# Four edits near the end of a fused forward-and-backward block: staging tiles, the order of three norms, filler matmuls, PSUM banks

## The chip, the cores and the metric

The kernel runs on one core of a Trainium2 chip. The metric is the time of one execution on the device in microseconds; of several runs the median counts. One run was also recorded by the hardware profiler; its page and its trace are what the readings below use. PE is TensorE, DVE is VectorE, ACT is ScalarE, POOL is GpSimd, SP is SyncE, which only issues DMAs here.

## The reference

The reference runs one block forward and then its gradient. The block has two halves, each with a layer norm that is scaled and shifted by vectors made from a condition `c`.

```python
mod = (silu(c) @ w_mod)            # sa, ca, ga, sb, cb, gb: six vectors of 576
h = layernorm(x) * (1 + ca) + sa
x = x + ga * irfft2(rfft2(h) * (w_r + 1j * w_i))          # half A, 2048 x 576
h = layernorm(x) * (1 + cb) + sb
x = x + gb * (((h @ w_gate) * (h @ w_up)) @ w_down)       # half B, 4608 hidden
# outputs: x, and the gradients of A_x, w_r, w_i, w_gate, w_up, w_down, c, w_mod
```

All inputs and outputs are bfloat16. The 2048 rows are 16 tiles of 128, the 4608 hidden columns 36 blocks of 128. The Fourier transforms are done as matmuls with tables of sines and cosines.

## The kernel before

The program has these parts, in the order of the trace. All engines work through their own queues in order; a planner at compile time orders each queue by priorities and estimated due times, except where the program ties instructions together (`in_order`, or `behind`, which puts what is issued inside it after a given instruction of the same engine).

1. **The head** (up to L581): the forward transform, filter and inverse of half A, and in its gaps the product of `grad_out` and `w_down`, stored as `ghhT_d`.
2. **The gated loop** (L759 to L787): for each of the 36 blocks the two forward products (`gup`), the sums for the input gradient (`u8p`, added in SBUF by DVE at L751), and three weight-gradient products of an earlier block (`u57p`, `product`). Each of these 108 products is 2 x 16 matmuls; ACT copies it into one of four slots of the staging tile `so4`, and from there it is stored, or transposed by a DMA on SP's queue (L655) and then stored.
3. **The last two blocks** (L788 to L804): their sums come tile by tile (L791), 8 matmuls for each of 16 tiles, and `summed[t]` is DVE's last addition for tile t. Their six products are `held`: 48 of the 192 matmuls go between the sums (`lead`), 144 are left over as fillers. The sixth product, of block 35, uses the fourth slot of `so4` and the fifth product the third; both are transposed into the tiles `wo_l`.
4. **Stage 1** (`t1_norm`, `t1_turn`, `t1_cols`, `t1_rows`, 19 steps): the gradient of the second norm and the forward transform of the gradient. `t1_norm(t)` works on DVE and ACT (`norm_back`) and makes `gxf`, which PE turns in `t1_turn(t)` one step later. The norms of tiles 0, 1 and 2 are put behind `summed[8]`, `summed[11]` and `summed[14]` on DVE. After each `gx` store POOL's queue may carry a load for the last product: five tiles `wd` of 7, 7, 7, 7 and 8 blocks of `w_down`, and four `hl` tiles of stored activations (L1090 to L1098). These tiles lie in memory that the gated loop's tiles had before; a load waits until all tiles under it are done with.
5. **Stage 2** (`t2_...`, 24 steps): filter and its gradient. **Stage 3**, the inverse (`t3_rows`, `t3_cols`, `t3_norm`, 18 steps): the inverse transform and the gradient of the first norm; `t3_norm` adds column sums into `csD` and `csE`.
6. **The output product** `u3p` (L1263 to L1303): for each of 16 row tiles and each half of 288 columns 36 matmuls into one PSUM bank; ACT copies it to `ob`, DVE makes the output tile, POOL stores it. The first ten tiles' 720 matmuls are fillers; the last six tiles' follow. Behind tiles 8 to 13 stand six *sections* (`section`): PE spreads a vector (`spp`), ACT copies it (`dmb`, two buffers) and scales it five times, SP loads a part of `w_mod` (`wmj`, two buffers), and DVE multiplies the two (`pr7`). When all six are done, DVE makes `gcd` and PE the last product `gcp`.

`deal` (L882) writes PE's order through stages 1 to 3: after the matmuls of each step it takes `q` fillers from a list that begins with the 144 held matmuls and goes on with `u3p`: 16 a step in stage 1, 12 in stage 2, 20 in step 0 of stage 3 and 14 in each of its other steps. When the list is empty no more are taken; fillers left over follow in the planner's order.

PSUM has eight banks. In the last three stages three are `ps_fp`, three are `ps_cs` (tags `csA`, `csB`, `csC`; `csD` takes the bank of `csA`, `csE` that of `csC`), and two are `ps_u3`, in turn for `u3p`.

Of the kernel before, what the change touches and what calls it, by code (L numbers as in the profile page):

```python
# [9 lines left out]
FP32 = mybir.dt.float32  # L10
BF = mybir.dt.bfloat16
# [10 lines left out]
D = 576  # L22
DP = 640
# [75 lines left out]
def build(ctx, tc, A_x, A_w_r, A_w_i, B_w_gate, B_w_up, B_w_down, c_in, w_mod, grad_out,  # L99
          out_0, out_1, out_2, out_3, out_4, out_5, out_6, out_7, out_8):  # L100
    nc = tc.nc
# [46 lines left out]
    def traced():  # L148
        return len(nc.cur_bb.bb.instructions)
# [6 lines left out]
    def followed(mm, act):  # L156
        then_act[mm.ins.name] = act.ins
# [102 lines left out]
    with ExitStack() as hs:  # L260
        def pool(name, bufs, side="left", space=None, stack=hs):
            kw = dict(name=name, bufs=bufs, reuse_waits="tile")
            if space is not None:
                kw["space"] = space
            else:
                kw["side"] = side
            return stack.enter_context(tc.tile_pool(**kw))
# [315 lines left out]
    with ExitStack() as ms:  # L583
# [14 lines left out]
        def ghb(t):  # L598
            return acc(t).bitcast(BF)[:, 0:D]

        with ExitStack() as bs:
            FBW = 2
            FBT = 4
            def bpool(name, bufs, space=None):
                kw = {} if space is None else dict(space=space)
                return bs.enter_context(tc.tile_pool(name=name, bufs=bufs, reuse_waits="tile", **kw))
# [7 lines left out]
            sop = bpool("sop", 1)  # L614
# [10 lines left out]
            nc.gpsimd.memset(dgb_l[:], 0.0)  # L625
            pend = []
            NSO = 4
            so4 = sop.tile([128, NSO, DP], BF, name="so4")
            nc.gpsimd.memset(so4[:, :, D:DP], 0.0)
            nso = [0]  # L630
            late_sp, unstored = [], []

            def u57_items(sf, rhs_n, done):
                so = so4[:, nso[0] % NSO, :]
                nso[0] += 1
                items = []
                for h in range(2):
                    pw = []

                    def item(h, t, pw=pw):  # L640
                        if t == 0:
                            pw.append(u57ps.tile([128, 512], FP32, name="u57p", tag="x"))
                        mm = nc.tensor.matmul(pw[0][:, 0:288], lhsT=sf[:, t, :], rhs=rhs_n(t, h * 288, 288), start=(t == 0), stop=(t == NT - 1))  # L643
                        if t == NT - 1:
                            followed(mm, nc.scalar.copy(so[:, h * 288:(h + 1) * 288], pw[0][:, 0:288]))  # L645
                            if h == 1:
                                done(so)
                    items += [lambda h=h, t=t, item=item: item(h, t) for t in range(NT)]
                return items
# [89 lines left out]
            summed = {}  # L739
# [70 lines left out]
    with ExitStack() as ts:  # L810
# [9 lines left out]
        ps_cs = pool("ps_cs", 1, space=PSUM)  # L820
        ps_u3 = pool("ps_u3", 2, space=PSUM)
# [37 lines left out]
        def behind(insts):  # L859
            es = ExitStack()  # L860
            for i_ in insts:
                es.enter_context(tc.issue_after(i_))
            return es
# [18 lines left out]
        def deal(held, proj):  # L882
            more, seq, acts = held + proj, list(lead), scaled["2"][0:3]
            for n, (stage, k, ins) in enumerate(staged):
                last_ = len(seq)
                seq += ins
                steps = sum(x[:2] == (stage, k) for x in staged)
                at = sum(x[:2] == (stage, k) for x in staged[:n + 1])
                q = 16 if stage == 1 else 12 if stage == 2 else 20 if k == 0 else 14
                q = q * at // steps - q * (at - 1) // steps  # L890
                seq, more = seq + more[:q], more[q:]
                if stage == 1:
                    acts += [then_act[i_.name] for i_ in seq[last_:] if i_.name in then_act]
                    acts += scaled["2"][k + 2:k + 3] * (at == steps and k > 0)
            in_order(seq)
            in_order(acts)
# [56 lines left out]
        with ExitStack() as r1:  # L953
# [14 lines left out]
            def t1_norm(t):  # L968
                if t == 0:
                    nc.sync.dma_start(ga_h[:], modb_d[:, MGA, :])  # L970
                for k, src, tt in [("n2c", n2_d, 0)] * (t == 0) + [("n2c", n2_d, t + 1)] * (t < NT - 1) + [("yc", y_d, t)]:
                    ld[k, tt] = c1.tile([128, D], BF, name=k, bufs=5 if k == "n2c" else 3)
                    with behind(ld["order"]):
                        ins = nc.sync.dma_start(ld[k, tt][:], src[:, tt, :])
                    ld[k, "ins", tt] = ins.ins
                if t in (1, 2):
                    ld["order"] = [ins.ins]
                    with behind(ld["order"]):
                        for k, tag in ((("RF", "tA"),), (("G1", "tB"), ("BD2", None), ("BDA", None)))[t - 1]:
                            T[k] = load_table(tl0, k, tag)  # L980
                    ld["order"] = [tab_ins[k]]
                n2 = ld["n2c", t][:]
                gh, gx = ghb(t), rings["gxr"][:, t % 4, 0:D]
                gn = c1.tile([128, D], BF, name="gn2")
                nc.vector.tensor_tensor(out=gn[:], in0=gh, in1=opcb_h[:], op=MUL)
                with behind([summed[8 + 3 * t]] if t < 3 else []):
                    norm_back(c1, gn, n2, rstd2g[:, t:t + 1], gon(t), gx, "2")
                ld["gx", t] = nc.gpsimd.dma_start(gx1_d[:, t, :], gx).ins
                gf = rings["gxf"][:, t % 3, :]
                nc.vector.tensor_tensor(out=gxa[:, 0:D], in0=gx, in1=ga_h[:], op=MUL)  # L990
                nc.vector.tensor_tensor(out=gf[:, 0:DF], in0=gxa[:, 0:DF], in1=gxa[:, D:DF - 2:-1], op=ADD)
                nc.vector.tensor_tensor(out=gf[:, DF:D], in0=gxa[:, 1:DF - 1], in1=gxa[:, D - 1:DF - 1:-1], op=SUB)
# [270 lines left out]
        for tp_ in range(NT // 2):  # L1263
            for nq in {4: range(16, 28), 5: (28, 29), 6: (30, 31)}.get(tp_, range(4 * tp_, 4 * tp_ + 4) if 0 < tp_ < 4 else ()):
                hls_of.setdefault(nq // 4, []).append(hl_load(nq, behind_=ld["yc", "ins", NT - 1]))
            hls = hls_of[tp_]
            x1t = o2p.tile([128, 2, D], BF, name="x1t3")
            with behind([last[nc.gpsimd]] if tp_ == 0 else []):
                x1l = nc.gpsimd.dma_start(x1t[:], x1_d[:, 2 * tp_:2 * tp_ + 2, :])
            if tp_ == 0:  # L1270
                last[nc.gpsimd] = x1l.ins
            obs = {}
            for group in [[(0, 0), (1, 0)], [(0, 1), (1, 1)]] if tp_ == 0 else [[(0, 0)], [(0, 1)], [(1, 0)], [(1, 1)]]:
                mark = traced()
                p2 = {}
                for ti, h in group:
                    p2[ti] = ps_u3.tile([128, 512], FP32, name="u3p")
                    if h == 0:
                        obs[ti] = o2p.tile([128, D], BF, name="ob3", bufs=4)
                for fb in range(NFB):  # L1280
                    f0, w = wd_part(fb)
                    mms = []
                    for ti, h in group:
                        mm = nc.tensor.matmul(p2[ti][:, 0:288], lhsT=hls[fb // 9][:, fb % 9, ti * 128:(ti + 1) * 128], rhs=w[:, fb - f0, h * 288:(h + 1) * 288], start=(fb == 0), stop=(fb == NFB - 1))  # L1284
                        mms.append(mm)
                for (ti, h), mm in zip(group, mms):
                    followed(mm, nc.scalar.copy(obs[ti][:, h * 288:(h + 1) * 288], p2[ti][:, 0:288]))
                proj += pe_since(mark) if tp_ < 5 else []
                for ti, h in group:
                    if h == 0:  # L1290
                        continue
                    t = 2 * tp_ + ti
                    of = o2p.tile([128, D], BF, name="of3", bufs=3)
                    nc.vector.tensor_tensor(out=of[:], in0=obs[ti][:], in1=gb_h[:], op=MUL)
                    nc.vector.tensor_tensor(out=of[:], in0=of[:], in1=x1t[:, ti, :], op=ADD)
                    stored = nc.gpsimd.dma_start(o0_v[:, t, :], of[:])
                    if t in late:
                        with behind([mm.ins, ld3["last"]]):
                            section(*late[t], secp)
                    more_grads(t)  # L1300
                    if 11 <= t < 15:
                        for k in range(4 * (t - 11), 4 * (t - 10)):
                            store_grads(k, stored.ins)  # L1303
# [74 lines left out]
```

## Time and profile before

| what | value |
| --- | --- |
| median of the runs | 1540.54 us (1538.65 to 1549.71) |
| profiled execution, whole | 1535.2 us |
| its span, first to last instruction | 1533.4 us |
| granted TensorE clock, mean | 0.996 |
| PE busy | 1494.3 us, 97% |
| DVE busy | 1060.9 us, 69% |
| ACT busy | 582.5 us, 38% |
| POOL busy | 237.3 us, 15% |

A row of the chain of waits has a start, a length and what ran then. A timeline row has start, length, engine, line, operation, output and inputs, and in brackets the idle time before it and what ended that. A row of windows has the stretch, its length, the busy time of PE, PEld (weight loads), DVE, ACT and POOL with their counts, the granted clock, the DMA share and GB/s. A row of waits says who waited for whom, for how long in all, how often, and the longest.

### The profile page before, as it was taken

Reading aid. Unit: us, or ns where it says so; the run is one execution under the profiler, and the core shown is the slowest. Engines: PE = TensorE matmul, PEld = TensorE weight load, DVE = VectorE, ACT = ScalarE, POOL = GpSimd, SP = SyncE. Lnnn points to the kernel's source line nnn. Section 1 sums busy time; section 2 is a strip of 40 time slices with the busy share of each in tenths; the row PEclk is TensorE's granted clock in tenths of the full one; section 3 lists DMA queues with packets and bytes.
Section 4 is the critical chain, followed back from the end, with each engine's and each line's share of the span. In section 5 each row is a group of like instructions: output and inputs, shape, how many; then the busy total and the mean of one; then the engine's idle time right before and its main releaser. Section 6 shows DMA issues by size and latency. Waiting matters only on the chain. (4 is left out here: it accounts for less than half of the span.)

```text
span 1533.4 us, 29027 instructions
## 1 busy us (share of the span) xinstructions
PE 1494.3 (97%) x11140; PEld 1012.6 (66%) x11144; DVE 1060.9 (69%) x2646; ACT 582.5 (38%) x1189; POOL 237.3 (15%) x360
## 2 busy tenths in 40 slices
PE   6899899999999999999999999999999999899998
PEld 4666543566666667666676666666766667788766
DVE  6866653666767767667677676776766677488874
ACT  6667742322222222222222222222222226586753
POOL 0001222101101111111120110110211113221022
PEclk9999999999999999999999999999999999999999
DMA  9868997588868768869788587876877779865586
GB/s 317 289 198 221 271 285 214 149 162 154 185 118 165 156 117 171 151 141 170 128 159 162 122 162 151 142 157 141 157 150 139 147 172 265 262 218 184 177 295 192
DMA packets 487181, 280.42 MB, mean 183 GB/s; under 512 B 408865, under 2 KB 457378, under 8 KB 486018
## 3 DMA queue, kind: packets, MB, share of 16 engines
q1 hardware_dynamic: 458882, 175.32, 54.5%
q0 software_dynamic: 28160, 103.25, 23.1%
q8 instruction: 87, 1.43, 0.4%
q14 instruction: 52, 0.43, 0.1%
HBM read 108.62 MB, written 82.31 MB: 125 GB/s over the span
## 5 line engine op out<-in xcount | busy, mean ns | idle before, releaser
L751 DVE TENSOR_TENSOR acc<-acc,u8p 128x288 f32<-128x288 f32 (+1 forms) x1088 | 483.5, 453 | 276.2 <-PE u8p L746 272.7
L746 PE MATMUL u8p<-wT,ggT 128*128 128x288 bf16 x1152 | 328.0, 286 | 2.4 <-DVE acc L751 2.3
L746 PE MATMUL u8p<-wT,guT 128*128 128x288 bf16 x1152 | 327.7, 286 | 0.0
L710 PE MATMUL gup<-h2T,wgu 128*128 128x512 bf16 x1152 | 297.9, 379 | 0.0
L645 ACT CAST so<-u57p 128x288 bf16<-128x288 f32 x216 | 86.0, 398 | 534.1 <-PE u57p L643 524.1
L643 PE MATMUL u57p<-h2p,gu_sf 128*128 128x288 bf16 x1152 | 186.4, 286 | 0.0
L643 PE MATMUL u57p<-h2p,gg_sf 128*128 128x288 bf16 x1152 | 185.9, 286 | 0.0
L1284 PE MATMUL u3p<-wd,hl 128*128 128x288 bf16 x1152 | 169.3, 289 | 6.7 <-DMA wd<-in_B_w_down_dram 3.9
L710 PEld LDWEIGHTS <-wgu 128*128 128x128 bf16 x1152 | 109.6, 98 | 97.9 <-issue 17.0
L746 PEld LDWEIGHTS <-ggT 128*128 128x128 bf16 x1152 | 112.6, 98 | 66.4 <-issue 14.0
L451 PE MATMUL u4p<-goT,wdT 128*128 128x512 bf16 x656 | 151.2, 379 | 1.6 <-DVE ghh_st L173 1.1
L746 PEld LDWEIGHTS <-guT 128*128 128x128 bf16 x1152 | 112.7, 98 | 58.4 <-issue 3.1
L712 ACT CAST gT<-gup 128x512 bf16<-128x512 f32 x144 | 84.3, 585 | 131.6 <-PE gup L710 129.7
L643 PEld LDWEIGHTS <-hh_sf 128*128 128x128 bf16 x1152 | 112.7, 98 | 28.4
L643 PEld LDWEIGHTS <-gu_sf 128*128 128x128 bf16 x1152 | 112.4, 98 | 28.5
L643 PEld LDWEIGHTS <-gg_sf 128*128 128x128 bf16 x1152 | 112.4, 98 | 28.2
L1284 PEld LDWEIGHTS <-hl 128*128 128x128 bf16 x1152 | 108.3, 99 | 33.5 <-issue 7.1
L712 ACT CAST uT<-gup 128x512 bf16<-128x512 f32 x144 | 84.3, 585 | 77.6 <-PE gup L710 77.6
L451 PEld LDWEIGHTS <-wdT 128*128 128x128 bf16 x656 | 61.2, 98 | 74.0 <-issue 8.7
L643 PE MATMUL u57p<-gonC,hh_sf 128*128 128x288 bf16 x576 | 99.7, 286 | 0.0
L723 POOL DMA_DIRECT2D hhT_d<-hhT x36 | 33.2, 922 | 375.4 <-DVE hhT L714 352.5
L173 DVE CAST ghh_st<-u4p 128x512 bf16<-128x512 f32 x56 | 38.7, 691 | 59.0 <-PE u4p L451 58.9
(371 smaller groups left out, 1837.5 us busy)
## 6 DMA issues: line engine op xcount, KB each, us to landing
ghhT_d<-ghh_st POOLq DMA_DIRECT2D x36, 512.0 KB, 4.2
ghh<-ghhT_d POOLq DMA_DIRECT2D x36, 512.0 KB, 7.4
hhT_d<-hhT POOLq DMA_DIRECT2D x36, 512.0 KB, 6.3
hl<-hhT_d SPq DMA_DIRECT2D x28, 576.0 KB, 5.7
out_dram<-woT SPq DMA_DIRECT2D x70, 128.0 KB, 2.0
wdn<-in_B_w_down_dram SPq DMA_DIRECT2D x18, 288.0 KB, 3.9
wd<-in_B_w_down_dram POOLq DMA_DIRECT2D x36, 144.0 KB, 4.7
out_dram<-so SPq DMA_DIRECT2D x36, 144.0 KB, 2.8
```

The costliest lines, as they stand in the source:

```text
L173: nc.vector.tensor_copy(dst, src)
L451: nc.tensor.matmul(pt[:], lhsT=wdTs[k][:, j, m, :], rhs=goT[:, 4 * sb4:4 * sb4 + 4, m, :], start=(m == 0 and n == 5), stop=(m == n - 1))
L643: mm = nc.tensor.matmul(pw[0][:, 0:288], lhsT=sf[:, t, :], rhs=rhs_n(t, h * 288, 288), start=(t == 0), stop=(t == NT - 1))
L645: followed(mm, nc.scalar.copy(so[:, h * 288:(h + 1) * 288], pw[0][:, 0:288]))
L710: nc.tensor.matmul(pts[k][:], lhsT=wgu[:, 4 * wi_ + m, jw * 128:(jw + 1) * 128], rhs=h2T[:, ts_, m, :], start=False, stop=(m == 3))
L712: nc.scalar.copy((gT, uT)[wi_][:, th_, :], pts[k][:])
L723: nc.gpsimd.dma_start(hhT_d[:, :, fb, :].rearrange("tp f x -> f tp x"), hhT[:].rearrange("f (tp ti) p -> f tp (ti p)", ti=2))
L746: nc.tensor.matmul(pu[:, 0:288], lhsT=l_, rhs=r_, start=(k == 0), stop=(k == len(mms) - 1))
L751: summed[t] = nc.vector.tensor_tensor(out=ghb(t)[:, hs_] if fbs[-1] == NFB - 1 else dst, in0=dst, in1=pu[:, 0:288], op=ADD).ins
L1284: mm = nc.tensor.matmul(p2[ti][:, 0:288], lhsT=hls[fb // 9][:, fb % 9, ti * 128:(ti + 1) * 128], rhs=w[:, fb - f0, h * 288:(h + 1) * 288], ...
```

## The change

Four edits. The staging tile `so4` with four slots becomes four tiles of one slot each, with a memset for each one's padding. The first three norms of stage 1 stand behind the sums of tiles 8, 12 and 15. Stage 3 takes 16 fillers a step where it took 14. And from tile 10 of the output product on, the second half of the columns goes into the banks `csA` (even tiles) and `csB` (odd tiles), while the first half stays with the two `u3p` banks.

```diff
             NSO = 4
-            so4 = sop.tile([128, NSO, DP], BF, name="so4")
-            nc.gpsimd.memset(so4[:, :, D:DP], 0.0)
+            so4 = [sop.tile([128, DP], BF, name="so%d" % k) for k in range(NSO)]
+            for so in so4:
+                nc.gpsimd.memset(so[:, D:DP], 0.0)
...
-                so = so4[:, nso[0] % NSO, :]
+                so = so4[nso[0] % NSO][:]
...
-                q = 16 if stage == 1 else 12 if stage == 2 else 20 if k == 0 else 14
+                q = 16 if stage == 1 else 12 if stage == 2 else 20 if k == 0 else 16
...
-                with behind([summed[8 + 3 * t]] if t < 3 else []):
+                with behind([summed[(8, 12, 15)[t]]] if t < 3 else []):
...
                 for ti, h in group:
-                    p2[ti] = ps_u3.tile([128, 512], FP32, name="u3p")
+                    n3 = 4 * tp_ + 2 * ti + h
+                    p2[ti] = ps_cs.tile([128, 512], FP32, name="u3q", tag="cs" + "AB"[n3 // 2 % 2]) if tp_ > 4 and n3 % 2 else ps_u3.tile([128, 512], FP32, name="u3p")
```

## The prediction

> **What bounds the kernel now.** I read the page's first part, who is busy:
>
> ```profile
> PE 1494.3 (97%) x11140; PEld 1012.6 (66%) x11144; DVE 1060.9 (69%) x2646; ACT 582.5 (38%) x1189; POOL 237.3 (15%) x360
> ```
>
> TensorE (PE) stands still for 3% of the span. The change adds no matmul and takes none away, so it can only move PE's idle time and PE's speed. The windows show both, from the last sums of the gated loop on (stretch, its length, busy us of PE, PEld, DVE, ACT, POOL, granted clock, DMA share, GB/s):
>
> ```profile
> 1240.00:1300.00 60.00, 56.39 (x511) 44.30 (x510) 49.52 (x138) 26.79 (x67) 14.70 (x21) 1.00 0.97 257
> 1300.00:1345.00 45.00, 40.85 (x384) 32.62 (x383) 23.49 (x67) 24.33 (x62) 11.18 (x22) 0.96 0.85 266
> ```
>
> The second has a lower clock beside its idle time. The view of waits, for PE from 1240 us on, names what it stood for (us in all, times, longest):
>
> ```profile
> PE u3p L1284 <- DMA wd<-in_B_w_down_dram: 3.9, 1, 3.9
> PE u3p L1284 <- ACT ob L1287: 2.8, 1, 2.8
> PE u8p L746 <- DVE acc L751: 2.3, 2, 2.0
> PE zp L1016 <- ACT b_Vp L1025: 1.2, 7, 0.2
> PE spp L926 <- ACT ye L1211: 0.5, 1, 0.5
> PE upb L212 <- ACT ye L1211: 0.4, 1, 0.4
> ```
>
> The first three make 9.0 us, and each stands at a place that one part of the change touches. The longest ones cost more than themselves, as PE comes back at half speed; behind the first:
>
> ```profile
> 1320.00:1322.00 2.00, 2.00 (x10) 1.25 (x9) 0.00 (x0) 0.09 (x1) 0.00 (x0) 0.50 0.04 15
> ```
>
> **Part A, four staging tiles.** The chain of waits leads into the 3.9 us (start, length, what):
>
> ```profile
> 1306.19 4.51 DMA wo_l<-so
> 1310.81 0.51 issue
> 1311.34 7.93 DMA wd<-in_B_w_down_dram
> 1319.31 2.08 PE u3p L1284 x8
> ```
>
> The fifth `wd` tile (blocks 28 to 35) takes memory in which the staging tile `so4` lay. In the compiled program `so4` has bytes 108000 to 113120 of each partition, 1280 for each slot, and `wd4` has 102432 to 111648: it covers slots 0, 1 and part of 2, but not 3. As `so4` is one tile, the load waits for the transposition out of slot 3 too: the 4.51 us above. With four tiles that wait falls away. What is late next is the transposition out of slot 2, from SP's timeline and the landing time of that one transfer:
>
> ```profile
> 1295.37 1.95 SPq L655 DMA_TRANSPOSE wo_l<-so  x1
> ```
>
> ```profile
> DMA to landing us min/median/max: 9.7/9.7/9.7
> ```
>
> It lands at 1295.37 + 9.7 = 1305.1. The load follows 0.65 us after its releaser now (1310.7 to 1311.34), so it would start near 1305.8. POOL stands at it from 1302.9 on:
>
> ```profile
> 1311.34 0.90 POOL L1063 DMA_DIRECT2D wd<-in_B_w_down_dram  x1 [8.43 <-ACT gyT L999]
> ```
>
> (1311.34 - 8.43; the ACT operation named had long been done.) The `gx` stores of the next tiles are queued behind it on POOL and move up with it. In 7.9 us the load lands at 1313.7. PE wants it at 1319.3 - 3.9 = 1315.4, so there are 1.7 us in hand. But slot 3's transposition (4.51 us) now runs beside it, and part B lets PE come earlier. The longest landing time of any transfer of this line bounds it from above:
>
> ```profile
> DMA to landing us min/median/max: 3.7/7.1/13.0
> ```
>
> At 13.0 it lands at 1318.8 and the stall shrinks by 0.5 alone. Gone with the stall is the half speed behind it, half of the 2.7 us from 1319.3 to 1322, 1.4. The bounds are thus 0.5 and 3.9 + 1.4 = 5.3; a loss is excluded, as the load waits for a part of what it waited for. I take 4.8, near the upper end, since 7.93 was measured for this very load, and leave 0.5 for its neighbours.
>
> The split also makes one memset four:
>
> ```profile
> 275.16 0.31 POOL L629 MEMSET so<- 128x256 bf16 x1 [2.38 <-PE u4p L451]
> ```
>
> Three more cost POOL under 1 us, in a place where it waits 2.38 us anyway; without that cover it would be 0.9 us late for one store. I count nothing.
>
> **Part B, the norms behind sums 8, 12, 15.** VectorE (DVE) adds each half of a sum from PSUM (`u8p`, three banks), and PE can run three halves ahead. The DVE timeline where PE stood 2.0 us:
>
> ```profile
> 1255.06 1.69 DVE L872 SCALAR_TENSOR_TENSOR w<-gn,rstd2g,n2c 128x576 bf16<-128x576 bf16 x1
> ...
> 1257.49 0.44 DVE L751 TENSOR_TENSOR acc<-acc,u8p 128x288 bf16<-128x288 f32 x1
> ```
>
> Right after the sum of tile 11 norm 1 starts, and 2.4 us go by to the next sum. Held behind tile 12, it starts two sums (2 x 0.44) later; DVE works two banks off first, so PE is 2 to 3 halves better placed when the same 2.4 us come. What queues behind the held norm on DVE is its own rest and norm 2, and PE's turn of `gxf` waits for these. For norm 2, now behind the last sum:
>
> ```profile
> 1267.69 0.29 DVE L992 TENSOR_TENSOR gxf<-gxa 128x287 bf16<-128x287 bf16 x1
> 1273.99 0.44 PE L997 MATMUL trp<-ident,gxf 128*128 128x128 bf16 x5
> ```
>
> Six microseconds of slack hide a delay of one tile's sums. The most to win is both waits, 2.3; the most to lose, if the planner sets norm 1 against the sums as badly one tile later and norm 2 adds its own share, is one such gap less one bank, about 1. I take a gain of 1.3, since DVE's total work stays and only its order moves.
>
> **Part C, 16 fillers in a step of the inverse stage.** Fillers are matmuls that stand in for idle time, and this stage has 0.9 us of it (the last two waits above). The supply is 144 held products and 720 matmuls of `u3p`. Stages 1 and 2 take 19 x 16 = 304 and 24 x 12 = 288, step 0 takes 20. Now 17 x 14 = 238 follow and 14 are left over. With 16 there are 252 for 17 steps: 15 full ones, 12 in step 16 and none in step 17. What these cover is the way from the last `yp` to the column sums, here in PE's timeline:
>
> ```profile
> 1457.63 0.92 PE L1208 MATMUL yp<-T_IF,ut 128*128 128x289 bf16 x6
> ...
> 1460.97 0.41 PE L907 MATMUL csE<-ghr,pick 128*128 128x288 bf16 x2
> ```
>
> That way is 1460.97 - 1458.55 = 2.4 us, and 0.5 to 1.6 us of it stay covered by four fillers and two pairs of `spp`. Cost: 0.8 to 1.9 us; it is 0 if matmuls of tile 10 slip in, and at best the 0.5 us wait for `spp` goes. I take a loss of 0.8. All else is a shift: the 28 matmuls (step 17's and those left over) after the column sums now come before them, so the sections start 28 x 8.82 / 72 = 3.4 us later against PE (rate from part D's row).
>
> **Part D, four banks.** `u3p` had two banks; from tile 10 on the second half goes to `csA` or `csB`. The ACT timeline of the 2.8 us wait:
>
> ```profile
> 1475.55 0.40 ACT L1287 CAST ob<-u3p 128x288 bf16<-128x288 f32 x1 [0.32 <-PE u3p L1284]
> 1484.27 0.70 ACT L938 COPY dmb<-spp 128x288 f32<-128x288 f32 x2 [8.32 <-DVE pr L951]
> 1485.00 3.56 ACT L945 ACTIVATE o<-dmb,sc_col 128x576 bf16<-128x576 f32 x5
> 1488.59 0.70 ACT L1287 CAST ob<-u3p 128x288 bf16<-128x288 f32 x2
> ```
>
> ACT stands 8.32 us before `dmb`, and tile 11's two banks wait behind it. With four, tile 12 opens on banks that tile 10 gave back by 1475.95. The stall goes, and with it the half speed. From the chain of waits:
>
> ```profile
> 1489.04 10.65 PE u3p L1284 x72
> 1499.69 0.97 PE spp L926 x4
> 1500.66 8.82 PE u3p L1284 x72
> ```
>
> 10.65 - 8.82 = 1.8 us, with 2.8 makes 4.6. The lower bound is nothing, if PE only reaches another late bank. `csA` is first free when `dca` has been read, behind the column sums; tile 10's first half (36 matmuls, 4.4 us) hides that. I take 4.2, near the upper end, as the first 0.4 may go on the first bank that comes late.
>
> The Trainium skill (TensorE: Matmul & The Clock Gate, Part 1) has the clock fall only when PE has been idle for a window of about 3.4 us. By that rule the second stall costs no half speed, part D is worth 2.8 at most, and the time is 1532.4. The trace disagrees:
>
> ```profile
> 1490.00:1492.00 2.00, 2.00 (x10) 1.22 (x9) 0.84 (x2) 2.00 (x4) 1.43 (x3) 0.50 1.09 293
> ```
>
> **Sum.** 4.8 + 1.3 - 0.8 + 4.2 = 9.5 us. The profiled execution took 1535.2 us around its span, so it would take 1525.7. It lies 5.3 below the median of the runs shown, 1540.5, so the runs' median would be **1531.0**. One per cent is 15.4 us, about what a measurement of this kernel can tell from no change.
>
> **The rivals.** (1) The wait only changes hands: `wd4` lands beside the transposition as late as the 13.0 row allows. For it: that transposition took 9.7 us beside another `wd`, and DMA shares stand at 0.97. Against: 7.93 measured. Part A gives 0.5: 1535.3.
>
> (2) The tail is held by the sections, not by PE:
>
> ```profile
> 1519.78 0.82 DVE L1310 TENSOR_TENSOR gcd<-ident,gcf 128x640 bf16<-128x640 bf16 x1
> ...
> 1528.40 0.21 DVE L1318 CAST gcr<-gcp 1x64 bf16<-1x64 f32 x1 [6.93 <-PE gcp L1314]
> ```
>
> ```profile
> 1480.00:1510.00 30.00, 27.23 (x199) 20.88 (x197) 17.40 (x45) 15.02 (x27) 8.03 (x12) 0.94 1.05 319
> ```
>
> From the column sums (over at 1461.4) the sections' chain of loads and products ends at 1520.6, 59.2 us on; PE hands over `gcp` at 1528.4, 67.0 on. Take off 3.4 for part C and 4.6 for part D, and PE needs 59.0: the chain binds by 0.2, and by more if its loads lengthen, where DMA is already full (1.05). Against: the 28 matmuls also free two `hl` slots earlier, so two loads leave the queue ahead of it. If D gives nothing, 1535.2.
>
> (3) Slower than before: nothing but the planner orders PE's queue after the inverse stage. With four banks it can put the groups of tiles 10 and 11 before the spreads that start the sections. Each tile put ahead delays the chain by 8.8 us. Against gains of 6.1 before the tail (A and B) and a slack of 7.8, it decides from 13.9 us on, which is two tiles: 1520.6 + 17.6 is 9.8 after the old hand-over, less 6.1, for 1544.2. For it: the order is free there. Against: the spreads are traced earlier, which ranks them ahead.
>
> (4) All upper bounds hold: 5.3 + 2.3 + 0.5 + 4.6 = 12.7, for 1527.8.
>
> **How the numbers follow.** Forecast 0.47, (1) 0.13, (2) 0.17, (3) 0.10, (4) 0.12, the page's rule 0.01. The runs shown spread over 11 us, so the range reaches 5 below (4), to 1523, and to just short of (3), 1543, where most of (3) is left out. Faster by over 1% (under 1525.1) takes (4) and a low median of the runs: 0.12. Slower by over 1% (over 1555.9) takes (3) with four tiles put ahead: 0.05. The rest, 0.83, is within 1%.
>
> **What would show it.** A: the `wd` load of POOL starts 5 to 6 us earlier against the `gx` store before it, and no wait of PE for `wd` is over 1 us. B: PE waits for `acc` under 1.3 us in all. C: no gap over 2 us around the last column sums, and no 28 matmuls behind them. D: no wait of PE for `ob`, and a clock of 1.00 up to the last tile. I am wrong if the PE wait for `wd` stays above 3 us, if a new wait over 2 us stands between 1455 and 1530, or if DVE reaches `gcd` after PE's last `u3p`.

## The result, and the profile after

The changed kernel takes 1526.36 us in the median of six runs (1522.84 to 1528.15), the kernel before, timed beside it, 1541.78 us (1533.74 to 1549.71). The ratio is 0.9896, with a 95% interval of 0.9861 to 0.9931: some 1% faster. The forecast was 1531.0 in a range of 1523 to 1543. The profiled execution took 1524.87 us around a span of 1523.1, which is 10.3 us less than the span before.

The first part of the page after, and the windows and PE's waits that answer to those shown of before:

```profile
PE 1490.3 (98%) x11140; PEld 1012.6 (66%) x11144; DVE 1060.6 (70%) x2646; ACT 583.4 (38%) x1189; POOL 238.8 (16%) x363
```

```profile
1240.00:1300.00 60.00, 57.05 (x525) 44.94 (x525) 50.16 (x139) 28.00 (x70) 15.41 (x22) 1.00 0.98 263
1300.00:1345.00 45.00, 44.95 (x446) 36.85 (x445) 26.31 (x76) 27.00 (x65) 13.56 (x26) 1.00 0.95 315
```

```profile
PE spp L927 <- ACT dmb L939: 2.4, 1, 2.4
PE u8p L747 <- DVE acc L752: 1.6, 2, 1.3
```

The waits for `wd` (3.9) and for `ob` (2.8) are gone, that for `acc` has become 0.7 shorter, and a new one stands in the list: PE waits 2.4 us with a spread, because the bank it needs is still to be copied by ACT into `dmb`. In the changed file a line has a number one or two higher than before; the files of the experiments keep the numbers of before.

The table cuts each profiled execution by PE's first and last instruction of a kind: head (start to the first `gup` product), loop (to the last `u8p`), stage 1 (to the turn of tile 12, the first turn behind the `wd` wait of before), to the last column sum `csE`, sections (to PE's end), tail (to the span's end). Every number is a difference of two such starts or ends, in us. The last two columns give the median of all runs (4 to 12 of them) and the ratio to the kernel before, timed beside it, with its interval.

| kernel | head | loop | stage 1 | to `csE` | sections | tail | without head | median | ratio |
|---|---|---|---|---|---|---|---|---|---|
| before | 275.0 | 986.6 | 62.5 | 137.9 | 66.3 | 5.1 | 1258.4 | 1541.8 | |
| A alone | 274.5 | 986.6 | 56.8 | 137.9 | 64.9 | 5.1 | 1251.3 | 1533.4 | 0.9947 (0.9919 to 0.9974) |
| B alone | 281.7 | 985.8 | 63.1 | 137.9 | 66.5 | 5.0 | 1258.4 | 1542.3 | 1.002 (0.9987 to 1.0052) |
| C alone | 272.9 | 986.6 | 67.9 | 137.9 | 62.3 | 7.4 | 1262.1 | 1537.5 | 0.9984 (0.9956 to 1.0013) |
| D alone | 275.0 | 986.6 | 64.9 | 137.9 | 62.0 | 9.0 | 1260.5 | 1538.3 | 1.0001 (0.9972 to 1.003) |
| A, B | 275.6 | 985.8 | 56.5 | 137.9 | 68.7 | 5.0 | 1254.1 | 1531.6 | 0.995 (0.9927 to 0.9974) |
| A, B, C | 276.7 | 985.9 | 56.5 | 138.0 | 63.0 | 7.0 | 1250.3 | 1534.3 | 0.9935 (0.9905 to 0.9966) |
| A, B, D | 271.5 | 985.8 | 56.5 | 137.9 | 62.8 | 7.7 | 1250.8 | 1525.7 | 0.9915 (0.9878 to 0.9953) |
| all four: the change | 272.8 | 985.9 | 56.5 | 138.0 | 62.6 | 7.3 | 1250.3 | 1526.4 | 0.9896 (0.9861 to 0.9931) |
| the change, 18 fillers | 274.5 | 985.9 | 56.5 | 138.9 | 59.3 | 6.4 | 1247.0 | 1526.0 | 0.988 (0.9841 to 0.9918) |
| the change, own bank | 278.0 | 985.8 | 56.5 | 138.0 | 63.5 | 5.9 | 1249.7 | 1527.5 | 0.9887 (0.9852 to 0.9922) |
| the change, late stores | 286.0 | 985.8 | 56.5 | 137.9 | 60.6 | 8.2 | 1249.1 | 1530.2 | 0.9942 (0.9916 to 0.9967) |
| own bank, late stores | 281.9 | 985.8 | 56.5 | 138.0 | 58.0 | 9.4 | 1247.8 | 1525.5 | 0.99 (0.9872 to 0.9928) |
| own bank, spread stores | 279.9 | 985.8 | 56.5 | 138.0 | 58.0 | 6.2 | 1244.6 | 1526.2 | 0.992 (0.9892 to 0.9949) |

Read the first column before any other. No part of the change touches the head, and it lasts from 271.5 to 286.0 us. In the two extremes, PE's waits from 150 to 250 us, for A, B, D first and the change with late stores second:

```profile
PE yp L216 <- ACT ut L171: 1.3, 1, 1.3
PE yp L216 <- DVE ut L173: 0.2, 1, 0.2
```

```profile
PE yp L216 <- DVE ut L173: 5.6, 3, 3.8
PE yp L216 <- ACT ut L171: 3.2, 3, 1.3
```

From 200 to 250 us the granted clock was 1.00 in the first and 0.90 in the second. So a median of a few runs of this kernel can't tell gains of 3 us apart, and the experiments below are read by the columns behind the head. By these the change is worth 8.1 us: loop 0.7, stage 1 6.0, sections 3.7, less 2.2 in the tail. The other 2.2 us of the span lie in the head. That the medians differ by 15.4 us, more than these 10.3, is left open: the profile of before (1535.2) was one of its shorter runs.

### The profile page after: what moved, and what is told of

Its sections match the earlier page's. It is cut to its first block, busy times and chain, and to the rows that moved or that the text cites. A ratio compares the mean times of both kernels' runs of the same rounds, so it can differ in the third digit from the quotient of the medians.

```text
span 1523.1 us, 29031 instructions
## 1 busy us (share of the span) xinstructions
PE 1490.3 (98%) x11140; PEld 1012.6 (66%) x11144; DVE 1060.6 (70%) x2646; ACT 583.4 (38%) x1189; POOL 238.8 (16%) x363
## 5 line engine op out<-in xcount | busy, mean ns | idle before, releaser
L747 PEld LDWEIGHTS <-ggT 128*128 128x128 bf16 x1152 | 112.6, 98 | 66.5 <-issue 14.0
L1286 PE MATMUL u3p<-wd,hl 128*128 128x288 bf16 x936 | 141.3, 288 | 0.1
```

The costliest lines, as they stand in the source:

```text
L747: nc.tensor.matmul(pu[:, 0:288], lhsT=l_, rhs=r_, start=(k == 0), stop=(k == len(mms) - 1))
```

## The experiments

### One part at a time

Part A alone:

```
-            so4 = sop.tile([128, NSO, DP], BF, name="so4")
+            so4 = [sop.tile([128, DP], BF, name="so%d" % k) for k in range(NSO)]
```

> The kernel before with part A alone (four staging tiles, all else as before). Theory 1 (the load is released early, and this is the change's largest gain): PE's wait of 3.9 us for the fifth wd tile is gone together with the half speed behind it, every mark of PE behind tile 11 of the gated loop lies 5 to 6 us earlier, and the time falls by 4 to 6 us (ratio near 0.997). Rival (the two traces differ there because parts B and C moved the DMA queues, and the split alone changes little): a wait of PE for wd of more than 2 us stays, and the time falls by less than 2 us. A second rival for the end: PE's end moves by 5 to 6 us, but the span moves by less than 3, because the tail is held by the sections' loads.

Stage 1 is 5.7 us shorter; theory 1 holds. On POOL the `wd` load started 8.98 us behind the `gx` store before it (at 1311.34, behind the first row here), and with A alone it starts 3.84 us behind it:

```profile
1302.36 0.55 POOL L988 DMA_DIRECT2D gx_d<-gxr  x1 [2.48 <-DVE gxr L880]
```

```profile
1301.80 0.55 POOL L988 DMA_DIRECT2D gx_d<-gxr  x1 [2.48 <-DVE gxr L880]
1305.64 0.90 POOL L1063 DMA_DIRECT2D wd<-in_B_w_down_dram  x1 [3.29 <-ACT zt L1017]
```

The time agrees with it (6 us in the medians); the rival for the end, a longer tail, did not come. The sections are 1.4 us shorter too, and that is not A's doing: the wait for `ob` was 2.2 us in this execution instead of 2.8, full speed followed it, and a wait of 0.8 us for `hl` was new.

Part B alone:

```
-                with behind([summed[8 + 3 * t]] if t < 3 else []):
+                with behind([summed[(8, 12, 15)[t]]] if t < 3 else []):
```

> The kernel before with part B alone (the first three norms behind the sums of tiles 8, 12 and 15). Theory 1: PE's waits for acc fall from 2.3 to about 1.6 us, the start of the turns of tile 0 lies 1.0 us earlier against the first product of the loop, and the time moves by 1 us, which the timing can't tell from no change. Rival (what the two traces show there came from the head of the kernel): the way from the first gup product to the first turn stays within 0.3 us of before.

```profile
PE u3p L1284 <- DMA wd<-in_B_w_down_dram: 5.0, 1, 5.0
...
PE u8p L746 <- DVE acc L751: 1.6, 2, 1.3
```

The waits for `acc` fall to 1.6 and the loop is some 0.7 us shorter, near theory 1. But PE then waits 5.0 us for `wd` instead of 3.9: what PE gains ahead of a late load it gives back at the load. Without A, B is worth nothing (1258.4 in both); beside A it is worth 1.0 up to the turn of tile 12 (0.7 in the loop, 0.3 in stage 1).

Part C alone:

```
-                q = 16 if stage == 1 else 12 if stage == 2 else 20 if k == 0 else 14
+                q = 16 if stage == 1 else 12 if stage == 2 else 20 if k == 0 else 16
```

> The kernel before with part C alone (16 fillers in a step of the inverse stage). Theory 1 (hidden idle: the step is set by a chain over DVE and ACT, 3.75 us a step, and PE has 0.25 us of idle in each step that the modelled ends of its matmuls cover): the steps stay 3.75 us long with two more fillers in each, the last column sums come no later than before although 28 more products lie before them, and the time falls by 3 to 4 us, less what the tail takes back. Rival (my prediction's reading: PE sets the step): the steps grow to about 4.0 us, the last column sums come 3.4 us later, and the time rises by 0.8 us.

```profile
PE csC L914 <- DMA yc<-y_d: 3.9, 1, 3.9
PE spp L926 <- ACT dmb L938: 2.5, 1, 2.5
```

The way to the last column sum is 137.9 us with and without the 28 further products in it (in the two traces 720 products of `u3p` start ahead of it, against 692); the sections behind it are 4.0 us shorter, of which 28 x 0.1225 = 3.4 are those products. Theory 1 holds. But the wait for `ob` has only changed hands: the spread's wait for `dmb` stands in its place, and without part D. The tail grows by 2.4, and in this execution PE stood for a late `yc` row in stage 1, far ahead of what C touches.

Part D alone:

```
-    p2[ti] = ps_u3.tile([128, 512], FP32, name="u3p")
+    n3 = 4 * tp_ + 2 * ti + h
+    p2[ti] = ps_cs.tile([128, 512], FP32, name="u3q", tag="cs" + "AB"[n3 // 2 % 2]) if tp_ > 4 and n3 % 2 else ps_u3.tile([128, 512], FP32, name="u3p")
```

> The kernel before with part D alone (four banks from tile 10 on). Theory 1 (the wait only changes hands): the wait of PE for ob (2.8 us) is gone, a wait of spp for dmb of 2 to 3 us stands in its place with a slow clock behind it, and the time moves by less than 1 us. Theory 2 (my prediction): no wait over 1 us in its place, and PE's end comes 4.2 us earlier. Theory 3 (the gain at PE is real but the sections' loads hold the end): PE's end comes 4 us earlier and the span less than 2 us.

PE's waits from 1455 us on:

```profile
PE spp L926 <- ACT ye L1211: 0.5, 1, 0.5
```

Nothing stands in the place of the wait for `ob`, and the sections are 4.3 us shorter, the wait and the half speed behind it: within a tenth of the prediction's 4.2, and theory 1 falls here. Yet the tail grows from 5.1 to 9.0 us, so the span keeps 0.4 of them. That is theory 3. DVE's waits behind 1480 us say why; before first, D alone second:

```profile
DVE pr L951 <- ACT dmb L938: 9.4, 1, 9.4
DVE gcr L1318 <- PE gcp L1314: 6.9, 1, 6.9
DVE pr L951 <- DMA wmj<-in_w_mod_dram: 2.6, 2, 1.4
```

```profile
DVE pr L951 <- DMA wmj<-in_w_mod_dram: 14.7, 4, 11.5
...
DVE gcr L1318 <- PE gcp L1314: 0.4, 1, 0.4
```

Before, DVE waited 6.9 us for PE at the end; with D it waits 0.4, and 14.7 for the sections' `wmj` loads. DVE ends together with PE, and POOL issues its last store 3.4 us behind PE's end, where before it was 1.45. (Stage 1 is longer here, 64.9, because the wait for `wd` was 5.2 us in this execution; D touches nothing there.)

### Taking parts out of the change

C taken out (14 fillers again):

> The changed kernel with 14 fillers in a step again (parts A, B and D without C). Theory 1 (C brings the start of the sections 3.4 to 3.7 us forward, and with that the third and fourth section meet a late dmb buffer; D's gain is real only without C): the last column sums come at the same distance from the turns as before, 28 products stand behind them, no wait of spp for dmb is over 1 us and none for ob, and PE's end lies within 1 us of the changed kernel's, counted from the first product of the gated loop; the span, held by the tail, is 0 to 3 us longer than the changed kernel's. Rival (the spp wait belongs to D's banks): the wait of spp for dmb of 2 to 3 us is there too, and PE's end comes 3.5 us later.

D taken out (two banks again):

> The changed kernel without part D (all u3p in two banks; parts A, B and C). Theory 1 (beside C, the wait for dmb stands in the place of the wait for ob, so that D has nothing left to give): the wait of spp for dmb of 2 to 3 us is there, no wait for ob of more than 1 us, and the time agrees with the changed kernel's within 1 us. Rival (D gives its 4 us in the changed kernel): PE waits for ob again and the time is 4 us longer.

C and D taken out:

> The changed kernel without C and without D (parts A and B). Theory 1 (C and D stand for each other at PE, and the sections' loads take what either gives): PE's end lies within 2 us of 202.8 us behind the turn of tile 12, as with A alone, the tail is 5 us long, the span ends within 1.5 us of 207.9 us behind that turn, and the time is 1 us below A alone. Rival (the medians of A alone, 1533.4, and of all four parts, 1526.4, tell a gain of 6 to 7 us from C and D together that the single profiles do not show): the time is 1532 to 1534 us, while the changed kernel's stays at 1526.

PE's waits from 1455 us on, in A B D, in A B C, and in A B:

```profile
PE u3p L1284 <- DMA hl<-hhT_d: 1.0, 1, 1.0
```

```profile
PE spp L926 <- ACT dmb L938: 2.5, 1, 2.5
PE u3p L1284 <- DMA hl<-hhT_d: 1.9, 2, 1.7
```

```profile
PE u3p L1284 <- ACT ob L1287: 3.6, 1, 3.6
```

In the profiles the expectations for A B D and A B C came true; the median of A B C did not agree with the change's within 1 us. The wait for `dmb` comes with C and not with D: C brings the spreads forward against a `dmb` buffer that becomes free only when DVE has multiplied the `wmj` of two sections earlier. ACT starts the copy in question 22.0 to 22.2 us behind the last column sum in before, in C alone, in A B C and in the change, however early PE comes.

From the last column sum to the span's end it is 73.7 us with neither, 70.0 with C, 70.5 with D, 69.9 with both: in these profiles the second part adds nothing to the first. But 73.7 is not the price of having neither, as A alone has neither and took 70.0. Its wait for `ob` was 2.2 us with full speed behind it; in A B the wait was 3.6 us, and half speed followed for 6.8 us:

```profile
1483.00:1489.82 6.82, 5.44 (x23) 3.45 (x23) 5.26 (x14) 5.73 (x11) 3.90 (x6) 0.50 0.90 275
```

So the stall that C or D takes away cost some 2 us in one execution and 6 in another (the last section says why). The expectation for A B, within 2 us of 202.8 behind the turn of tile 12, was missed by this: 206.7. The medians put D higher (A B C 1534.3, A B D 1525.7, A B 1531.6) than the single profiles do; why the runs of A B C were mostly longer than its profile, 1528.8, is open.

### How much idle time the inverse stage holds

```
-  20 if k == 0 else 16
+  20 if k == 0 else 18
```

> The changed kernel with 18 fillers in a step of the inverse stage: 14 full steps and none in the last three. Theory 1 (the step is set by a chain over DVE and ACT of 3.75 us and PE's hidden idle is used up with 16): the full steps grow to 3.95 to 4.05 us, the steps without fillers stay near 3.75, the last column sums come 2.5 to 3.5 us later, and the time rises by 1 to 3 us. Rival (PE still has idle time in the step): the steps stay at 3.76 us and the column sums come no later. My prediction's reading (PE set the step all along, even with 14): the steps were 3.76 us long by chance; with 18 they are 3.76 + 2 x 0.122 = 4.0 us as in theory 1, but then the changed kernel's 16 would have shown steps of 4.0 where it shows 3.76.

DVE starts the same operation once in each step. Six of them in before (14 fillers), in the change (16), and with 18:

```profile
L1222 DVE TENSOR_TENSOR gn<-ghr,opca_h x6: 458/459/460, 1418.4 to 1437.4; 128x576 bf16<-128x576 bf16 x6
```

```profile
L1223 DVE TENSOR_TENSOR gn<-ghr,opca_h x6: 459/459/460, 1409.8 to 1428.8; 128x576 bf16<-128x576 bf16 x6
```

```profile
L1222 DVE TENSOR_TENSOR gn<-ghr,opca_h x6: 458/459/460, 1411.9 to 1431.9; 128x576 bf16<-128x576 bf16 x6
```

Five steps take 19.0, 19.0 and 20.0 us: 3.8, 3.8 and 4.0 a step. Two fillers more cost nothing up to 16, and 0.2 us beyond. The idle time that 14 left is in PE's timeline, but no view calls it idle. One step of before, then one of the change:

```profile
1439.65 0.60 PE L210 MATMUL upa<-T_GB,j_A 128*128 128x256 bf16 x4
1440.24 0.27 PE L212 MATMUL upb<-T_GB,j_At 128*128 128x128 bf16 x2
...
1440.96 0.50 PE L907 MATMUL csE<-ghr,pick 128*128 128x288 bf16 x2
1441.30 0.38 PE L914 MATMUL csD<-n1c,ghr 128*128 128x128 bf16 x4
```

```profile
1408.41 0.60 PE L210 MATMUL upa<-T_GB,j_A 128*128 128x256 bf16 x4
1408.85 0.27 PE L212 MATMUL upb<-T_GB,j_At 128*128 128x128 bf16 x2
...
1409.70 0.41 PE L908 MATMUL csE<-ghr,pick 128*128 128x288 bf16 x2
1409.94 0.39 PE L915 MATMUL csD<-n1c,ghr 128*128 128x128 bf16 x4
```

From `upa` to `upb` it is 0.59 us before and 0.44 after, from `csE` to `csD` 0.34 and 0.24: 0.25 us less, two fillers of 0.1225 (8.82 / 72). A record lasts longer than the distance to the next one, so a gap of 0.1 us between them is covered by the record's own end. What sets the step instead is, as far as the rows show, DVE's chain over ACT, here in before:

```profile
1439.94 0.46 DVE L880 TENSOR_TENSOR ob<-u,w 128x576 bf16<-128x576 bf16 x1 [0.57 <-ACT w L877]
...
1443.69 0.46 DVE L880 TENSOR_TENSOR ob<-u,w 128x576 bf16<-128x576 bf16 x1 [0.58 <-ACT w L877]
```

DVE stands for ACT's `w` once a step, and `ob` follows `ob` after 3.75 us. The expectation that the column sums come 2.5 to 3.5 us later was wrong: they came 1.0 later (138.9), as the last steps, with 7 and 3 fillers left for them, took 3.1 and 2.75 us from `csE` to `csE`. In the last one DVE makes `ghr` ahead of `ob` and stands for no `w`, so 3.75 us belongs to the order of DVE's queue and is no floor. Nor did the time rise. The sections were 3.3 us shorter: the wait for `dmb` was 2.12 us and PE came back at full speed, worth some 2.0, and 732 products of `u3p` lie ahead of the last column sum instead of 720, worth 12 x 0.1225 = 1.5.

### What holds the end

The second spread of the `dgb` section gets the bank of the column sums, free by then:

```
-            pp = ps_fp.tile([128, 512], FP32, name="spp", tag="fp")
+            pp = ps_cs.tile([128, 512], FP32, name="spq", tag="csC") if own else ps_fp.tile([128, 512], FP32, name="spp", tag="fp")
```

> The changed kernel with the second spread of the dgb section in a bank of its own (the one of the column sums, free by then). Theory 1 (the wait of 2.4 us is for a spp bank, and PE queues behind it): the wait of PE for dmb is gone with the slow clock behind it, PE's end comes 3 to 4 us earlier, but the span gains only 0 to 2 us, because the end then hangs on the sections' loads and on the stores that POOL issues last. Rival (the next bank is as late): a wait of PE for ob or spp of 2 us or more stands within 10 us of the place, and PE's end moves by less than 1 us.

PE's waits from 1455 us on:

```profile
PE u3p L1284 <- DMA hl<-hhT_d: 3.4, 2, 2.7
```

The wait for `dmb` is gone, the next spread came 4.4 us earlier (167.2 us behind the turn of tile 12, 171.5 in the change), and PE ran into the last two `hl` loads: the sections last 63.5 us, against 62.6. The rival has it, with a load in the place of a bank. In the change, too, the transfers of that place were full and slow:

```profile
1490.00:1492.00 2.00, 2.00 (x19) 1.58 (x17) 1.10 (x4) 1.88 (x3) 2.00 (x4) 1.00 1.04 211
```

Eight stores of `wn` stand among these loads. They were moved behind tile 13:

```
-                    for k in range(4 * (t - 11), 4 * (t - 10)):
+                    for k in range(*{11: (0, 0), 12: (0, 0), 13: (0, 12), 14: (12, 16)}[t]):
```

> The changed kernel with the eight stores of wn that POOL issues between the loads of the last hl and wmj tiles moved behind the product tile 13 (12 stores there, 4 behind tile 14, none before). Theory 1 (from 1480 us on the transfers are the bound, and these stores delay the two last loads of hl and the two last of wmj): DVE's wait of 12.0 us for wmj shrinks by 2 to 5 us, PE's end stays (its wait for dmb is untouched), and the tail behind PE's end falls from 7.3 to 5 to 6 us, so that the time falls by 1 to 2 us. Rival (POOL's queue holds the end): the stores now stand together at the end, the last store of out_0 comes no earlier, and the time stays or rises by up to 3 us.

> The changed kernel with three edits: the second dgb spread in a bank of its own, the wn stores late as in the run before, and the last store of out_0 on SP's queue. Theory 1 (the bank's 3.7 us were lost to the late hl loads alone): PE waits under 1.5 us for hl, PE's end lies 196 to 198 us behind the turn of tile 12 (200.6 in the changed kernel, 201.4 with the bank alone), the tail behind it is 5 to 6 us, and the time is 4 to 6 us under the changed kernel's. Rival (the transfers bind by their sum, not by their order): PE still waits 2 us or more for hl, and the time is within 2 us of the changed kernel's.

With the stores alone, this is DVE's wait for the sections' loads:

```profile
DVE pr L951 <- DMA wmj<-in_w_mod_dram: 6.5, 2, 5.7
```

The longest one fell from 12.0 to 5.7 us. PE's end came 2.1 us earlier, but that is not the stores': PE's wait for `dmb` was 2.30 us instead of 2.40, with full speed behind it. The tail, which was to become shorter, took 0.9 back, as POOL now issues twelve stores in a row. With the bank too, the sections last 58.0 us, 4.6 less than in the change, and PE waits for nothing behind the loop but 1.2 us in stage 2. The last two `hl` loads landed after 5.5 and 6.0 us, where with the bank alone it took 11.3 and 13.7. So the order of the transfers was to blame, not their sum. But the tail grew to 9.4 us, and of the 4 to 6 us that were expected of the time the median shows 0.8:

```profile
1508.87 7.82 POOL L1257 DMA_DIRECT2D out_dram<-wn  x11
...
1518.74 0.56 POOL L1296 DMA_DIRECT2D out_dram<-of  x1 [1.15 <-DMA out_dram<-wn]
```

(The second of the two runs has the last `out_0` store on SP's queue as well.) Last, the stores in two rows of eight, behind tiles 12 and 13, and the `out_0` stores of tiles 14 and 15 on SP's queue:

```
-    for k in range(*{11: (0, 0), 12: (0, 0), 13: (0, 12), 14: (12, 16)}[t]):
+    for k in range(*{11: (0, 0), 12: (0, 8), 13: (8, 16), 14: (0, 0)}[t]):
-    stored = (nc.gpsimd if t < NT - 1 else nc.sync).dma_start(o0_v[:, t, :], of[:])
+    stored = (nc.gpsimd if t < NT - 2 else nc.sync).dma_start(o0_v[:, t, :], of[:])
```

> The three edits of the bank_late run with the stores of wn spread otherwise: 8 behind tile 12 (after the last hl loads are issued), 8 behind tile 13, and the stores of out_0 of tiles 14 and 15 both on SP's queue. Theory 1 (with PE free of waits, what is left behind its end is POOL's row of late stores: 0.72 us an issue and 6 to 7 us to landing): PE's end stays at 196 to 197 us behind the turn of tile 12, the tail falls from 9.4 to 5 to 6 us, the span ends 202 us behind that turn (205.4 in bank_late, 207.9 in the changed kernel), and the time falls 3 us under bank_late's, to about 1522.5. Rival (the 8 stores at tile 12 delay the last wmj and hl loads again): PE waits for hl for over 1 us or DVE reaches gcd behind PE's last product, and the time is no better than bank_late's.

The span ends 202.2 us behind the turn of tile 12, as expected (202), and 5.7 us earlier than in the change. The medians don't show it: 1526.2, where 1522.5 was expected, and a ratio of 0.992 (0.9892 to 0.9949), no better than the change's. No version was shown to beat the change.

## Why the prediction was right, and where it was wrong

The total was forecast as 9.5 us. The profiled span fell by 10.3, of which the parts gave 8.1 and a head that nobody had touched 2.2. That the two numbers are so near is luck. C and D were forecast as a loss of 0.8 and a gain of 4.2, together 3.4, and gave 3.7 at PE; but alone they gave 4.0 and 4.3, and the second beside the first almost nothing. The tail, which the sum put at nothing, lost as much as the head happened to win.

**A**, 4.8 forecast, 5.7 measured: over its upper bound of 5.3. The start of the load was right (5 to 6 us earlier), and its landing time too: 8.4 us beside the 8.6 us transposition of slot 3, against 7.93. Mis-sized was the half speed. The prediction counted it from 1319.3 to 1322; it lasted to 1322.63:

```profile
1319.22:1322.63 3.41, 3.33 (x14) 2.02 (x14) 0.26 (x2) 0.64 (x2) 0.00 (x0) 0.50 0.09 31
```

That is 0.3 us more, 5.6 in all. Rival (1) did not come.

**B**, 1.3 forecast, 1.0 measured, but "PE waits for `acc` under 1.3 us in all" failed (1.6), and its gain hangs on A, which the sum did not say.

**C**, a loss of 0.8 forecast, a gain of 4.0 at PE measured where it is alone. The step that failed is "this stage has 0.9 us of it": idle time was read from the view of waits, which showed none because the ends of the matmul records cover it. There were 0.25 us in each step, where 28 products found room for nothing. The range reached up to a gain of 0.5 only.

**D**, 4.2 forecast: 4.3 at PE where it is alone, 0.2 to 0.4 at PE in the change (63.0 to 62.6). The step that failed is adding D to C. Both end the wait for `ob`, so beside C there is none left for D; and with C the spread's bank is late, 2.4 us and a slow clock behind it:

```profile
1472.59 0.65 PE L927 MATMUL spp<-dgb,ones_f 128*128 128x288 f32 x2
1475.64 1.19 PE L927 MATMUL spp<-dgb,ones_f 128*128 128x288 f32 x2 [2.40 <-ACT dmb L939]
1476.62 5.85 PE L1286 MATMUL u3p<-wd,hl 128*128 128x288 bf16 x36
```

```profile
1475.18 0.70 ACT L939 COPY dmb<-spp 128x288 f32<-128x288 f32 x2 [6.40 <-DVE pr L952]
```

"A new wait over 2 us between 1455 and 1530" was named as what would make the prediction wrong, and it came. The ACT row shown for D had the warning in it: ACT stood 8.32 us before that very `dmb`, and the prediction moved only what queued behind it.

**The tail** lost 2.2 us. This comes out as rival (2) said, with the end held behind the sections' loads and not by PE, but in another place than the chain to `gcd` that it named. On DVE, then on POOL:

```profile
1503.16 0.76 DVE L952 SCALAR_TENSOR_TENSOR pr<-wmj,dmb 128x576 bf16<-128x576 bf16 x1 [12.02 <-DMA wmj<-in_w_mod_dram]
```

```profile
1514.85 2.83 POOL L1258 DMA_DIRECT2D out_dram<-wn  x4
1517.68 0.56 POOL L1298 DMA_DIRECT2D out_dram<-of  x1
```

DVE waits 12.0 us for `wmj`, so the product of tile 14 is formed late behind the sections' work, and the last store stands behind four of `wn` on POOL. It is issued 1.86 us behind PE's end, where before it was 1.45, and takes 3.9 us to land, where it took 2.1: together the 2.2 us. DVE reached `gcd` at 1512.3, still 3.5 us ahead of PE's end at 1515.8, so that sign was the wrong one to watch: POOL's queue came last. Rival (3) did not come; the spreads kept their place.

## What to carry to other kernels

Idle time of TensorE between short matmuls shows in no view of waits or busy time: compare the distance between starts with the same instructions elsewhere, or add fillers until the step grows. Two edits that end the same stall are not worth their sum, and each stall removed is followed on to the next resource, here from PE's banks to `dmb`, to `hl` and `wmj`, to POOL's row of stores. Cut a profile into stretches at marks and compare those: a head that scatters by 14 us hides what a change of 3 us does.

## What the runs showed of the hardware

The half speed comes in stretches of a fixed length. In the 14 traces the granted clock changes only at the marks of a grid of 3.41 us, which lies differently in each execution. What counts is how long PE stands still within one stretch of the grid, not how long a wait is. In the change the wait of 2.40 us falls into one stretch; in A B C a wait of 2.47 us is split over two. Both cut at the grid, the change first:

```profile
1472.40:1475.81 3.41, 1.01 (x6) 0.53 (x5) 3.27 (x9) 0.63 (x2) 0.53 (x1) 1.00 1.00 387
1475.81:1479.22 3.41, 3.41 (x13) 2.02 (x14) 3.20 (x10) 3.35 (x6) 0.00 (x0) 0.50 0.74 221
```

```profile
1475.14:1478.55 3.41, 1.92 (x14) 1.21 (x12) 3.27 (x10) 0.00 (x0) 1.66 (x3) 1.00 1.07 395
1478.55:1481.97 3.42, 2.44 (x18) 1.88 (x19) 3.28 (x9) 2.86 (x6) 0.00 (x0) 1.00 0.83 267
1481.97:1485.38 3.41, 3.41 (x30) 2.73 (x28) 2.56 (x8) 3.33 (x7) 0.30 (x1) 1.00 0.77 256
```

In the change PE was busy for 1.01 of 3.41 us, and the next stretch ran at half speed, which costs 1.7 us; in A B C it was busy for 1.92 and 2.44 us, and full speed went on. All 14 traces cut so, from 20 us on, show one limit: 34 stretches at full clock have 2.13 us or more without PE, and half speed follows each; the 6111 others have at most 1.97, and it follows none. So the waits of 2.12 us (18 fillers) and 2.30 us (late stores), both split, cost nothing more, and one of 2.35 us for `wd` in C alone, with 2.2 us in one stretch, did. A stretch at half speed was followed by another where PE stood for 0.97 us or more in it, as in A B, and not where it was 0.51 or less.

The Trainium skill (TensorE: Matmul & The Clock Gate, Part 1) has the clock fall after an idle window of about 3.4 us. The length agrees with the 3.41 us here; that the whole window has to be idle does not, as 2.13 us in it were enough.
